# The second output-weight tile of a gated MLP, split in two and laid at other byte offsets

## The chip, the cores and the metric

The kernel runs on one core of a Trainium2 chip, in float32. The time is that of one execution on the device, in microseconds. The profile is one further execution, recorded by the hardware profiler; its span runs from the first to the last instruction that it shows. The engines are named as in the profile: PE multiplies matrices, PEld is its loading of weights (the operand that stays in the array, 128 columns at a time, while the other one streams past), DVE and ACT work on vectors, POOL and SP here mostly issue DMA transfers.

## What is computed

A linear attention feeds a gated MLP. Shapes: q, k, v are 8 x 8 x 576 x 64; the MLP has 4608 tokens, width 512, hidden width 1536. The weights arrive as 64-bit floats and are narrowed on the chip.

```python
def _attn_ref(q, k, v):
    q_s = np.exp(q - np.max(q, axis=-1, keepdims=True))
    q_s = q_s / (np.sum(q_s, axis=-1, keepdims=True) + 1e-09)
    k_s = np.exp(k - np.max(k, axis=2, keepdims=True))
    k_s = k_s / (np.sum(k_s, axis=2, keepdims=True) + 1e-09)
    kv = np.einsum('bhsd,bhse->bhde', k_s, v)
    return np.einsum('bhsd,bhde->bhse', q_s, kv)

def _moe_ref(x, w_gate, w_val, w_out):          # x: attention, as 4608 x 512
    gate = 1.0 / (1.0 + np.exp(-(x @ w_gate)))
    return (gate * (x @ w_val)) @ w_out
```

## The kernel before

The tokens go in nine windows of 512 (T). Window 0 multiplies in plain float32 while the weights are read and prepared (g1_0 at L672, g2_0 at L699). Windows 1 to 8 multiply in float32r, a form in which a matmul streams its 512 columns faster; to keep the precision each operand is held as a high part and a low part, and a product is three matmuls: high by high, and high by low both ways.

Each of these windows has six steps, one for each pair of hidden blocks of 128 columns (NS = 6, step, at, p). A step has these parts, in program order:

- g1 (L717): the first layer for this pair, 84 matmuls of 256 columns in seven products (a Strassen scheme, prod). Its weights are a_w, which stays in SBUF, and s_sb, sums of weights that POOL loads again for the next step as each product is done (s_load, L301). What streams is c_hl, the window's attention output.
- On ACT and DVE: sigmoid, gate times value, and h_split (L767, L768), which makes the high and the low part of the pair's hidden values, h.
- side_a and side_b: attention work for the next window, some of it on PE (k_mm at L424 between g1 and g2 in one step of a window, x_mm at L587 behind g2 in the last).
- g2 (L785) of the step before: the second layer, 24 matmuls of 512 columns. For both blocks of the pair (i), for each of four token blocks (m), three matmuls. The operand that is loaded as weights is a 128-column slice of h; what streams is the output weights of that block, wo_hl for the first block and wo_t for the second.
- wo_load (L248), on POOL's queue: the output weights for the next step. Two tiles of 512 KB, each [128, 2, 512]: high part, then low part. The first comes from whpool (named wo_hl in the profile), the second from wtpool (wo_t). Each pool has two buffers, so a step is loaded while another is in use. The first step of window 1 takes both of its tiles from whpool, straight from where they were made (wo_out).

PE takes its matmuls in program order; the schedule is written by hand (manual_schedule). In window 0, wtpool also holds the narrowed output weights in float32 (wo_top, wo_join, two blocks to a tile), from which wo_hi and wo_lo make the high and the low part and wo_store sends them to DRAM (wo_dram).

What matters for the change is where in SBUF a tile begins. The pools lie one behind another in the order in which they are opened. The tiles of all pools around the change are multiples of 512 bytes per partition, and three pads stand between them: pad_w (128 bytes) in wpad, pad_h (128) in hpad, pad_f (64) in fpad. So, modulo 512, wo_t begins 128 bytes behind h, wo_hl 256 behind h, and the ring of attention tiles 320. h, a_w, s_sb and kv_sb, which are loaded as weights, all begin at the same place modulo 512; c_hl begins 448 bytes behind it. The slices that a matmul loads or streams start at multiples of 512 within their tiles, so each has its tile's offset.

Of the kernel before, what the change touches and what calls it, by code (L numbers as in the profile page):

```python
# [8 lines left out]
F32 = mybir.dt.float32  # L9
F32R = mybir.dt.float32r  # L10
# [4 lines left out]
ALU = mybir.AluOpType  # L15
AX = mybir.AxisListType

P = 128
B, H, S, D = 8, 8, 576, 64
DM, DF = 512, 1536  # L20
# [6 lines left out]
NJ = DF // P  # L27
NK = DM // P
NS = NJ // 2
# [22 lines left out]
def attn_moe(ctx: ExitStack, tc: tile.TileContext, qf, qn, qT, k, kT, v, wg, wv, wo, out):  # L52
    nc = tc.nc
# [8 lines left out]
    apool = ctx.enter_context(tc.tile_pool(name="apool", bufs=1))  # L62
    two = ctx.enter_context(tc.tile_pool(name="two", bufs=2))
    wpad = ctx.enter_context(tc.tile_pool(name="wpad", bufs=1))
    wtpool = ctx.enter_context(tc.tile_pool(name="wtpool", bufs=2))
    hpad = ctx.enter_context(tc.tile_pool(name="hpad", bufs=1))
    whpool = ctx.enter_context(tc.tile_pool(name="whpool", bufs=2))
    fpad = ctx.enter_context(tc.tile_pool(name="fpad", bufs=1))
    four = ctx.enter_context(tc.tile_pool(name="four", bufs=4))
# [19 lines left out]
    wo_dram = [spool.tile([P, 2 * DM], F32, name=f"wo_{j}") for j in range(NJ)]  # L89
# [3 lines left out]
        out=kv_sb.rearrange("p b i h e -> p (b i) (h e)"),  # L93
        in_=kv_0.rearrange("p h e -> p (h e)").unsqueeze(1).broadcast_to([P, 4, DM]),
# [19 lines left out]
    wo_raw = {}  # L114
    f_w = {}
    a_w = {}
    wo_t = {}
# [22 lines left out]
    def words(raw):  # L140
        return raw.rearrange("p (e two) -> p e two", two=2)
# [8 lines left out]
    def narrow_sign(raw):  # L150

        half = raw.bitcast(F16).rearrange("p (e f) -> p e f", f=4)
        nc.scalar.activation(
            half[:, :, 1], words(raw)[:, :, 1].bitcast(F32), AF.Copy, scale=2.0 ** -100
        )
# [8 lines left out]
    def narrow_abs(raw, w):  # L164
        src = words(raw)[:, :, 1].bitcast(F32)
        if len(w.shape) == 3:
            src = src.rearrange("p (a b) -> p a b", a=w.shape[1])
        nc.scalar.activation(w, src, AF.Abs, scale=2.0 ** -112)

    def narrow_join(raw, w):  # L170
        bits = w.bitcast(I32)
        low = words(raw)[:, :, 0]
        if len(w.shape) == 3:
            low = low.rearrange("p (a b) -> p a b", a=w.shape[1])
        nc.vector.scalar_tensor_tensor(
            out=bits, in0=bits, scalar=3, in1=low,
            op0=ALU.logical_shift_left, op1=ALU.bitwise_or,
        )
# [23 lines left out]
    def wo_on_vector(j):  # L202
        return j % 2
# [4 lines left out]
            narrow_sign_bits(wo_raw[j])  # L208

    def wo_top(j):  # L210
        if j % 2 == 0:
            wo_t[j // 2] = wtpool.tile([P, 2, DM], F32, name="wo_t")
        if not wo_on_vector(j):
            narrow_sign(wo_raw[j])
        narrow_abs(wo_raw[j], wo_t[j // 2][:, j % 2])

    def wo_join(j):
        narrow_join(wo_raw.pop(j), wo_t[j // 2][:, j % 2])

    wo_out = {}  # L220

    def wo_hi(j):
        wo_out[j] = t = whpool.tile([P, 2, DM], F32R, name="wo_hl")
        nc.scalar.copy(out=t[:, 0], in_=wo_t[j // 2][:, j % 2])

    def wo_lo(j):
        t = wo_out[j]
        nc.vector.tensor_tensor(
            out=t[:, 1], in0=wo_t[j // 2][:, j % 2], in1=t[:, 0].bitcast(F32), op=ALU.subtract
        )  # L230

    def wo_store(j):
        t = wo_out[j]
        nc.gpsimd.dma_start(out=wo_dram[j], in_=t.rearrange("p h e -> p (h e)").bitcast(F32))
# [5 lines left out]
    wo_hl = {}  # L240

    def wo_load(w, p):
        wo_hl[w, p] = [
            pool.tile([P, 2, DM], F32R, name=tag)
            for pool, tag in ((whpool, "wo_hl"), (wtpool, "wo_t"))
        ]
        for i, t in enumerate(wo_hl[w, p]):
            nc.gpsimd.dma_start(  # L248
                out=t.rearrange("p h e -> p (h e)"), in_=wo_dram[2 * p + i].bitcast(F32R)
            )  # L250

    s_32 = {}

# [401 lines left out]
    def c_split(i):  # L655
        c_split_hi(i)
        c_split_lo(i)


    acc = {}  # L660


    h_0 = {}
# [22 lines left out]
    def acc_new(w):  # L686
        acc[w] = [ps_acc.tile([P, DM], F32, name="acc") for _ in range(NT)]

    def acc_out(w):
        for m in range(NT):  # L690
            nc.scalar.copy(out=x_32[:, m], in_=acc[w][m])  # L691
            nc.sync.dma_start(out=out[w * T + m * P:w * T + (m + 1) * P], in_=x_32[:, m])
        del acc[w]

    def g2_0(j):
        if j == 0:
            acc_new(0)
        for m in range(NT):
            nc.tensor.matmul(  # L699
                acc[0][m], lhsT=h_0[j][:, m * P:(m + 1) * P], rhs=wo_t[j // 2][:, j % 2],  # L700
                start=(j == 0), stop=(j == NJ - 1),
            )
        if j == NJ - 1:
            acc_out(0)
# [57 lines left out]
    def h_split(w, p):  # L762
        h_hl[w, p] = hi, lo = [
            two.tile([P, 2, T], F32R, name="h", tag=f"h_{x}") for x in ("hi", "lo")
        ]
        hi, lo = (t.rearrange("p i (q t) -> p (i q) t", q=2) for t in (hi, lo))
        nc.vector.tensor_copy(out=hi, in_=sg[:, :, 0])  # L767
        nc.vector.tensor_tensor(  # L768
            out=lo, in0=sg[:, :, 0], in1=hi.bitcast(F32), op=ALU.subtract
        )  # L770


    def step(w, i):
        return (i - 1) % NS if w == 1 else i

    def g2(w, at):
        p = step(w, at)
        if at == 0:
            acc_new(w)
        h, o = h_hl.pop((w, p)), wo_hl.pop((w, p))  # L780
        for i in range(2):
            for m in range(NT):
                sl = slice(m * P, (m + 1) * P)
                for lh, rh in ((0, 0), (0, 1), (1, 0)):
                    nc.tensor.matmul(  # L785
                        acc[w][m], lhsT=h[lh][:, i, sl], rhs=o[i][:, rh],
                        start=(at == 0 and i == 0 and lh == 0 and rh == 0),
                        stop=(at == NS - 1 and i == 1 and lh == 1),
                    )
        if at == NS - 1:  # L790
            acc_out(w)
# [3 lines left out]
    def side_a(n, p):  # L795

        b = n if n < B else None
        if p == 0:
            for c in range(NC):
                qn_max(n, c)  # L800
            qn_send(n, "m")
            for c in range(NC):
                qn_sub(n, c)
            if b is not None:
                k_sub(b, 0); k_sub(b, 1)
                k_sum(b, 2); k_sum(b, 3)
        if p == 1:
            if b is not None:
                for t in range(2, 5):
                    k_sub(b, t)  # L810
            for c in range(NC):
                qn_exp(n, c)
            if b is not None:
                for t in range(5):
                    k_exp(b, t)
            for c in range(NC):
                qn_sum(n, c)
        if p == 2:
            if b is not None:
                for t in range(5):  # L820
                    k_mm(b, t)
                k_done(b)
            for hp in range(NP):
                qT_sub(n, hp)
        if p == 3:
            for hp in range(NP):
                qT_exp(n, hp)
        if p == 4:
            for hp in range(NP):
                qT_split(n, hp)  # L830
# [193 lines left out]
    for j in range(NJ - 2):  # L1024
# [31 lines left out]
        if j > 0:  # L1056
            g2_0(j - 1)
# [4 lines left out]
    j = NJ - 2  # L1062
# [15 lines left out]
    g_mul_0(j)  # L1078
    wo_join(j + 1)
    g2_0(j - 1)  # L1080

    g1_0(j + 1)
# [22 lines left out]
    wo_hi(j + 1)  # L1105
    wo_lo(j + 1)
    g2_0(j)
    for t in range(2, 5):
        v_load(2, t)

    def wo_next(w, at):
        wo_load(w, step(w, at))

    prev = None
    for w in range(1, NW):
        last = w == NW - 1
        for at in range(NS):
            p = step(w, at)
            end = last and at == NS - 1
            g1(w, p, None if end else step(w + (at + 1) // NS, (at + 1) % NS))  # L1120
            if prev is None:
                wo_store(NJ - 1)
            ahead = 3 if at == NS - 1 and not last else 0
            for i in range(ahead):
                c_split(i)
            h_split(w, p)
            if ahead:
                for i in range(ahead, 7):
                    c_split(i)
            if not last:  # L1130
                side_a(w + 1, at)
            if prev is None:
                g2_0(NJ - 1)
                wo_hl[1, NS - 1] = [wo_out[j] for j in (NJ - 2, NJ - 1)]
            else:
                g2(*prev)
                if prev == (1, 0):
                    wo_next(1, 1)
                if not end:
                    wo_next(w + (at + 1) // NS, (at + 1) % NS)  # L1140
            prev = (w, at)
            if not last:
                side_b(w + 1, at)
    g2(*prev)


# [36 lines left out]
```

## Time and profile before

| | |
|---|---|
| time, median of 3 runs | 928.67 us (928.15 to 929.54) |
| the profiled execution's own time | 928.82 us |
| its span | 927.1 us |
| instructions | 16312 |
| PE busy with L785, wo_hl (588 matmuls) and wo_t (564) | 142.6 and 138.9 us |
| PE busy with L717, s_sb (2304) and a_w (1728) | 277.5 and 220.9 us |
| DMA | 256.77 MB, mean 277 GB/s |

A row of the timeline gives the start of a group in us from the span's start, the time from its first start to its last end, the engine, the line, the operation, the tiles that it writes and reads, the shapes and the count. Matmuls overlap: each one's recorded duration is longer than its distance to the next, so a pace is read from starts. A row of the chain of waits gives start, duration and what ran. In a grouped row, busy time and the mean duration of one (in ns) stand behind the first bar, the engine's idle time ahead of it behind the second. A row of waits names who waited, for whom, the sum in us, how often, and the longest.

### The profile page before, as it was taken

Reading aid. Unit: us, or ns where it says so; the run is one execution under the profiler, and the core shown is the slowest. Engines: PE = TensorE matmul, PEld = TensorE weight load, DVE = VectorE, ACT = ScalarE, POOL = GpSimd, SP = SyncE. Lnnn points to the kernel's source line nnn. Section 1 sums busy time; section 2 is a strip of 40 time slices with the busy share of each in tenths; the row PEclk is TensorE's granted clock in tenths of the full one; section 3 lists DMA queues with packets and bytes.
Section 4 is the critical chain, followed back from the end, with each engine's and each line's share of the span. In section 5 each row is a group of like instructions: output and inputs, shape, how many; then the busy total and the mean of one; then the engine's idle time right before and its main releaser. Section 6 shows DMA issues by size and latency. Waiting matters only on the chain.

```text
span 927.1 us, 16312 instructions
## 1 busy us (share of the span) xinstructions
PE 919.4 (99%) x6366; PEld 793.9 (86%) x6366; DVE 619.1 (67%) x1005; ACT 488.7 (53%) x830; POOL 177.2 (19%) x329
## 2 busy tenths in 40 slices
PE   8999999999999999999999999999999999999998
PEld 7445445899999999999999999999999999899997
DVE  7899889865768476757775677656855574654232
ACT  5999885735454544644564456444634443543222
POOL 0011113222121212121221222112211222122220
PEclk9999999999999999999999999999999999999999
DMA  9996676999799969996999699969997799768661
GB/s 331 380 376 255 238 269 238 360 340 283 205 373 323 273 192 372 334 281 183 360 342 282 200 333 333 300 203 310 334 298 219 222 260 317 227 190 257 209 206 68
DMA packets 92507, 256.77 MB, mean 277 GB/s; under 512 B 13648, under 2 KB 13648, under 8 KB 92432
## 3 DMA queue, kind: packets, MB, share of 16 engines
q0 software_dynamic: 46016, 167.27, 57.8%
q1 hardware_dynamic: 46416, 88.48, 31.5%
q8 instruction: 50, 0.82, 0.4%
q14 instruction: 25, 0.20, 0.1%
HBM read 227.15 MB, written 28.56 MB: 276 GB/s over the span
## 4 chain that ended last, share of the span: by engine, by line
PE 98%; DMA 1%; SPq 0%; ACT 0%; issue 0%
PE gv L717 49%; PE acc L785 29%; PE gv L672 9%; PE acc L699 4%; PE at L424 2%; PE gv L587 2%; PE at L587 1%; DMA lent<-v_in 1%; DMA lent<-qf_in 1%; PE gv L549 0%; PE acc L611 0%; PE acc L410 0%; PE at L410 0%; SPq L948 0%; SPq L951 0%; ACT x L691 0%
## 5 line engine op out<-in xcount | busy, mean ns | idle before, releaser
L717 PE MATMUL gv<-c_hl,s_sb 128*128 128x256 f32 x2304 | 277.5, 276 | 0.0
L717 PEld LDWEIGHTS gv<-c_hl,s_sb 128*128 128x128 f32 x2304 | 269.0, 188 | 0.0
L717 PE MATMUL gv<-c_hl,a_w 128*128 128x256 f32 x1728 | 220.9, 277 | 0.0
L717 PEld LDWEIGHTS gv<-c_hl,a_w 128*128 128x128 f32 x1728 | 210.4, 188 | 4.6 <-issue 0.7
L301 POOL DMA_DIRECT2D s_sb<-s x188 | 101.7, 541 | 305.6 <-PE gv L717 297.9
L785 PE MATMUL acc<-wo_hl,h 128*128 128x512 f32 x588 | 142.6, 391 | 0.0
L743 DVE TENSOR_TENSOR sg<-gv,sg 128x512 f32<-128x512 f32 x48 | 33.2, 691 | 158.8 <-PE gv L717 158.8
L785 PE MATMUL acc<-wo_t,h 128*128 128x512 f32 x564 | 138.9, 394 | 0.0
L785 PEld LDWEIGHTS acc<-wo_t,h 128*128 128x128 f32 x564 | 105.8, 188 | 24.8
L785 PEld LDWEIGHTS acc<-wo_hl,h 128*128 128x128 f32 x588 | 106.9, 188 | 20.5
L735 ACT COPY sg<-gv 128x512 f32<-128x512 f32 x48 | 28.1, 586 | 111.0 <-PE gv L717 97.7
L745 ACT COPY sg<-gv 128x512 f32<-128x512 f32 x48 | 28.2, 588 | 102.7 <-PE gv L717 102.7
L747 DVE TENSOR_TENSOR sg<-sg 128x512 f32<-128x512 f32 x48 | 33.3, 693 | 57.3 <-ACT sg L745 57.3
L672 PE MATMUL gv<-x,f_w 128*128 128x512 f32 x160 | 70.4, 593 | 0.0
L248 POOL DMA_DIRECT2D wo_hl<-wo x47 | 27.7, 590 | 182.6 <-PE acc L785 182.6
L672 PEld LDWEIGHTS gv<-x,f_w 128*128 128x128 f32 x160 | 30.0, 190 | 36.6 <-issue 34.4
L768 DVE TENSOR_TENSOR h<-sg,h 128x1024 fp32r<-128x1024 f32 x48 | 58.9, 1226 | 1.6
L756 DVE TENSOR_TENSOR sg<-sg 128x512 f32<-128x512 f32 x48 | 33.3, 693 | 33.6 <-ACT sg L750 33.6
L750 ACT ACTIVATE sg<-sg 128x512 f32<-128x512 f32 x48 | 30.4, 633 | 46.1 <-DVE sg L749 46.1
L740 ACT COPY sg<-gv 128x512 f32<-128x512 f32 x48 | 28.2, 588 | 37.3 <-PE gv L717 37.3
L737 ACT COPY sg<-gv 128x512 f32<-128x512 f32 x48 | 28.2, 588 | 36.3 <-PE gv L717 36.3
L248 POOL DMA_DIRECT2D wo_t<-wo x47 | 25.4, 540 | 99.1 <-PE acc L785 99.0
(148 smaller groups left out, 1120.8 us busy)
## 6 DMA issues: line engine op xcount, KB each, us to landing
s_sb<-s POOLq DMA_DIRECT2D x188, 512.0 KB, 6.4
wo_hl<-wo POOLq DMA_DIRECT2D x47, 512.0 KB, 4.3
wo_t<-wo POOLq DMA_DIRECT2D x47, 512.0 KB, 6.1
s<-s_sb POOLq DMA_DIRECT2D x24, 512.0 KB, 6.9
out<-x SPq DMA_DIRECT2D x36, 256.0 KB, 6.9
ring<-k_in SPq DMA_DIRECT2D x28, 256.0 KB, 8.8
ring<-qn_in SPq DMA_DIRECT2D x28, 256.0 KB, 5.9
q_b<-q_m_row SPq DMA_DIRECT2D x56, 128.0 KB, 9.6
```

Source lines behind the costliest of these rows:

```text
L248: nc.gpsimd.dma_start(out=t.rearrange("p h e -> p (h e)"), in_=wo_dram[2 * p + i].bitcast(F32R))
L301: nc.gpsimd.dma_start(out=s_sb[:, i].rearrange("p h n e -> p (h n e)"), in_=s_dram[p][:, i * n:(i + 1) * n].bitcast(F32R),)
L672: nc.tensor.matmul(ps[n], lhsT=w[:, kt // 2, sl], rhs=x_0[:, kt], start=(kt == 0), stop=(kt == NK - 1),)
L699: nc.tensor.matmul(acc[0][m], lhsT=h_0[j][:, m * P:(m + 1) * P], rhs=wo_t[j // 2][:, j % 2], start=(j == 0), stop=(j == NJ - 1),)
L717: nc.tensor.matmul(ps[:, n], lhsT=lh(kt), rhs=c_hl[i][:, x, kt], start=(first and n == 0 and kt == 0 and lh is wh and x == 0), stop=(last ...
L737: nc.scalar.copy(out=sg[:, 2], in_=z)
L743: nc.vector.tensor_tensor(out=sg[:, 0], in0=rr, in1=sg[:, 0], op=ALU.add)
L747: nc.vector.tensor_tensor(out=sg[:, 3], in0=sg[:, 3], in1=sg[:, 2], op=ALU.add)
L750: nc.scalar.activation(sg[:, 0:2, 0], sg[:, 0:2, 0], AF.Sigmoid)
L756: tt(out=sg[:, 0:2, 0], in0=sg[:, 0:2, 0], in1=sg[:, 0:2, 1], op=ALU.mult)
L768: nc.vector.tensor_tensor(out=lo, in0=sg[:, :, 0], in1=hi.bitcast(F32), op=ALU.subtract)
L785: nc.tensor.matmul(acc[w][m], lhsT=h[lh][:, i, sl], rhs=o[i][:, rh], start=(at == 0 and i == 0 and lh == 0 and rh == 0), stop=(at == NS - ...
```

## The change

The second tile of a step's output weights becomes two tiles of [128, 512]: its high part, still from wtpool (wo_t), and its low part from a new pool, wlpool (wo_l). The pools are opened in another order: wpad, wlpool, hpad, wtpool, whpool. Modulo 512, wo_l then begins 128 bytes behind h, and wo_t and wo_hl 256. wo_load issues three transfers for a step instead of two. In g2 the order of the three matmuls changes for both blocks, so that the one with the low part of the output weights comes last, where it stood second. In window 0 the even blocks of the narrowed weights lie in wtpool, the odd ones in wlpool, instead of two to a tile.

```diff
     wpad = ctx.enter_context(tc.tile_pool(name="wpad", bufs=1))
+    wlpool = ctx.enter_context(tc.tile_pool(name="wlpool", bufs=2))
+    hpad = ctx.enter_context(tc.tile_pool(name="hpad", bufs=1))
     wtpool = ctx.enter_context(tc.tile_pool(name="wtpool", bufs=2))
-    hpad = ctx.enter_context(tc.tile_pool(name="hpad", bufs=1))
     whpool = ctx.enter_context(tc.tile_pool(name="whpool", bufs=2))
...
     def wo_top(j):
-        if j % 2 == 0:
-            wo_t[j // 2] = wtpool.tile([P, 2, DM], F32, name="wo_t")
+        pool, name = ((wtpool, "wo_t"), (wlpool, "wo_l"))[j % 2]
+        wo_t[j] = pool.tile([P, DM], F32, name=name)
         if not wo_on_vector(j):
             narrow_sign(wo_raw[j])
-        narrow_abs(wo_raw[j], wo_t[j // 2][:, j % 2])
+        narrow_abs(wo_raw[j], wo_t[j])
...
     def wo_load(w, p):
-        wo_hl[w, p] = [
-            pool.tile([P, 2, DM], F32R, name=tag)
-            for pool, tag in ((whpool, "wo_hl"), (wtpool, "wo_t"))
+        t = whpool.tile([P, 2, DM], F32R, name="wo_hl")
+        nc.gpsimd.dma_start(
+            out=t.rearrange("p h e -> p (h e)"), in_=wo_dram[2 * p].bitcast(F32R)
+        )
+        parts = [
+            pool.tile([P, DM], F32R, name=name) for pool, name in ((wtpool, "wo_t"), (wlpool, "wo_l"))
         ]
-        for i, t in enumerate(wo_hl[w, p]):
+        for h, o in enumerate(parts):
             nc.gpsimd.dma_start(
-                out=t.rearrange("p h e -> p (h e)"), in_=wo_dram[2 * p + i].bitcast(F32R)
+                out=o, in_=wo_dram[2 * p + 1][:, h * DM:(h + 1) * DM].bitcast(F32R)
             )
+        wo_hl[w, p] = [[t[:, h] for h in range(2)], parts]
...
-                for lh, rh in ((0, 0), (0, 1), (1, 0)):
+                for lh, rh in ((0, 0), (1, 0), (0, 1)):
                     nc.tensor.matmul(
-                        acc[w][m], lhsT=h[lh][:, i, sl], rhs=o[i][:, rh],
+                        acc[w][m], lhsT=h[lh][:, i, sl], rhs=o[i][rh],
                         start=(at == 0 and i == 0 and lh == 0 and rh == 0),
-                        stop=(at == NS - 1 and i == 1 and lh == 1),
+                        stop=(at == NS - 1 and i == 1 and rh == 1),
                     )
...
-                wo_hl[1, NS - 1] = [wo_out[j] for j in (NJ - 2, NJ - 1)]
+                wo_hl[1, NS - 1] = [
+                    [wo_out[j][:, h] for h in range(2)] for j in (NJ - 2, NJ - 1)
+                ]
```

wo_join, wo_hi, wo_lo and g2_0 read wo_t[j] in place of wo_t[j // 2][:, j % 2].

More of the change, by code (lines that the diff above doesn't have):

```diff
@@ L210, in wo_top @@
     def wo_top(j):
-        if j % 2 == 0:
-            wo_t[j // 2] = wtpool.tile([P, 2, DM], F32, name="wo_t")
+        pool, name = ((wtpool, "wo_t"), (wlpool, "wo_l"))[j % 2]
+        wo_t[j] = pool.tile([P, DM], F32, name=name)
         if not wo_on_vector(j):
             narrow_sign(wo_raw[j])
-        narrow_abs(wo_raw[j], wo_t[j // 2][:, j % 2])
+        narrow_abs(wo_raw[j], wo_t[j])
     def wo_join(j):
-        narrow_join(wo_raw.pop(j), wo_t[j // 2][:, j % 2])
+        narrow_join(wo_raw.pop(j), wo_t[j])
     wo_out = {}
@@ L223, in wo_hi @@
         wo_out[j] = t = whpool.tile([P, 2, DM], F32R, name="wo_hl")
-        nc.scalar.copy(out=t[:, 0], in_=wo_t[j // 2][:, j % 2])
+        nc.scalar.copy(out=t[:, 0], in_=wo_t[j])
     def wo_lo(j):
@@ L228, in wo_lo @@
         nc.vector.tensor_tensor(
-            out=t[:, 1], in0=wo_t[j // 2][:, j % 2], in1=t[:, 0].bitcast(F32), op=ALU.subtract
+            out=t[:, 1], in0=wo_t[j], in1=t[:, 0].bitcast(F32), op=ALU.subtract
         )
@@ L699, in g2_0 @@
             nc.tensor.matmul(
-                acc[0][m], lhsT=h_0[j][:, m * P:(m + 1) * P], rhs=wo_t[j // 2][:, j % 2],
+                acc[0][m], lhsT=h_0[j][:, m * P:(m + 1) * P], rhs=wo_t[j],
                 start=(j == 0), stop=(j == NJ - 1),
```

## The prediction

> **What bounds the kernel now.** I read the page first: share of each engine, granted clock, chain.
>
> ```profile
> span 927.1 us, 16312 instructions
> PE 919.4 (99%) x6366; PEld 793.9 (86%) x6366; DVE 619.1 (67%) x1005; ACT 488.7 (53%) x830; POOL 177.2 (19%) x329
> PEclk9999999999999999999999999999999999999999
> PE 98%; DMA 1%; SPq 0%; ACT 0%; issue 0%
> ```
>
> The matrix engine works from end to end at its full granted clock, and the chain that ended last is PE for 98%. Then the waits of PE, all of them:
>
> ```profile
> PE acc L394 <- ACT lent L337: 2.2, 2, 1.9
> PE gv L975 <- POOL lent L943: 1.1, 1, 1.1
> PE at L410 <- DMA lent<-v_in: 0.3, 1, 0.3
> ```
>
> 3.6 us in total, all in the prologue. So no load, no VectorE step and no buffer holds PE up in the 48 steps; what is left to win or lose is the pace at which matmuls follow each other. A busy PE hides that, so I read starts in the timeline. One step of the middle (start, duration, count; durations overlap, so the start of the next row is what counts):
>
> ```profile
> 405.41 2.90 PE L785 MATMUL acc<-wo_hl,h 128*128 128x512 f32 x12
> 408.15 2.95 PE L785 MATMUL acc<-wo_t,h 128*128 128x512 f32 x12
> 410.94 1.52 PE L717 MATMUL gv<-c_hl,a_w 128*128 128x256 f32 x12
> 412.30 2.88 PE L717 MATMUL gv<-c_hl,s_sb 128*128 128x256 f32 x24
> ...
> 420.46 2.90 PE L785 MATMUL acc<-wo_hl,h 128*128 128x512 f32 x12
> ```
>
> The twelve matmuls of the first tile (wo_hl, 256 bytes behind the weights modulo 512) take 408.15 - 405.41 = 2.74 us, the twelve of the second (wo_t, 128 behind) 410.94 - 408.15 = 2.79 us: 228.3 against 232.5 ns each, for the same work and the same shapes. The first step of the window loop has both of its tiles in wo_hl:
>
> ```profile
> 178.96 5.62 PE L785 MATMUL acc<-wo_hl,h 128*128 128x512 f32 x24
> 184.42 1.58 PE L717 MATMUL gv<-c_hl,a_w 128*128 128x256 f32 x12
> ```
>
> 5.46 us for 24, 227.5 each, against 5.53 in the step above. The offset is thus worth up to 0.07 us a step, and 47 steps have it: 3.3 us is all that the second tile can lose. But the chain of waits shows what follows that step (start, duration, what):
>
> ```profile
> 179.13 5.46 PE acc L785 x24
> 184.58 9.89 PE gv L717 x84
> 197.10 5.78 PE acc L785 x24
> 202.88 9.52 PE gv L717 x84
> 212.40 5.53 PE acc L785 x24
> 217.93 9.52 PE gv L717 x84
> ...
> 902.47 9.52 PE gv L717 x84
> ```
>
> The next product of the first layer (L717, 84 matmuls, the same in every step) takes 9.89 us behind the step that ended at 256 and 9.52 behind steps that ended at 128, with no wait in either. In the timeline its first twelve take 185.83 - 184.42 = 1.41 us against 412.30 - 410.94 = 1.36. So the pace has a memory: a run of matmuls settles into a rhythm that the end of the run before chose, and keeps it.
>
> **How the pace goes, matmul by matmul.** The rows above merge twelve starts. Read singly in the trace, they repeat to the nanosecond. In wo_hl behind L717 they lie 231, 233, 231 and then nine times 226.7 ns apart (2.735 us, the 2.74 of the row). In wo_t they lie 234 and 224, and then alternate 237.5 and 229 (2.79 us). The tail shows that going back from 128 to 256 costs what coming from L717 costs:
>
> ```profile
> 914.56 2.96 PE L785 MATMUL acc<-wo_t,h 128*128 128x512 f32 x12
> 917.35 2.90 PE L785 MATMUL acc<-wo_hl,h 128*128 128x512 f32 x12
> 920.09 2.96 PE L785 MATMUL acc<-wo_t,h 128*128 128x512 f32 x12
> ```
>
> 920.09 - 917.35 is 2.74 again, 0.015 us over twelve steady ones, all in the first three. The starts also show what state is carried: each falls on one of a few places in a beat of 6.67 ns (226.7 is 34 beats, 237.5 + 229 is 70), and the place and the offset decide the next distance.
>
> **The change, part by part.**
>
> *Offsets.* Of the 12 second-tile matmuls of a step, 8 move to 256 and 4 stay at 128, in the order 256, 256, 128, four times. The first tile only changes the order of its products; both h tiles are at one offset, so its pace stays. Priced by each matmul's own offset: 8 x 226.7 + 4 x 232.5 = 2.744 us for 2.79, 0.046 us a step. But a change of offset has a price too, and there are seven instead of one. A pair at 256 that comes from 128 is the first two of the tail's entry, 231 + 233 = 464 instead of 453; a 128 behind it takes 229 from the place where that entry stands after two. That round (231.7, 232.5, 229.2) closes on itself, at 104 beats: 693 ns for three, where wo_t now takes 3 x 233.3 = 700. The first three start from the steady 256: 226.7 x 2 + 234 = 687. Sum: 13 ns for the first and 6.7 for each of the other three, 0.033 us, or 0.026 if the second three must first find the round. I take 0.026, since the trace has no 256 right behind a single 128: 47 x 0.026 = 1.2 us less. Bounds: 47 x 0.07 = 3.3 us less if 128 costs nothing among 256s, a little more if its 224 comes back (four times 224 for 226.7, another 0.5 us); and if every second-tile matmul goes at the worst of its pairs, (238 + 234 + 233)/3 = 235 for 232.5, 47 x 12 x 2.5 ns = 1.4 us more.
>
> *What runs behind.* L717 now starts behind a 128 in steady alternation; of the 39 products that follow an L785 directly, 38 take the 9.52 pace (the first of them at 202.88, the last at 902.47; 184.58 is the other). In the round above the last 128 ends on the same place of the beat as now, so I leave L717 at 9.52. Seven times a run, attention products (L587) stand between:
>
> ```profile
> 236.41 9.89 PE gv L717 x84
> 332.98 9.55 PE gv L717 x84
> 811.83 9.89 PE gv L717 x84
> ```
>
> Two of the seven leave L717 slow today, and a new start may flip any: from 2 x 0.37 = 0.7 us less to 5 x 0.35 = 1.8 more. Taken as nothing.
>
> *The third transfer.* Each load of a step becomes three issues on POOL instead of two, 47 x 0.54 us, behind the end of L785:
>
> ```profile
> 411.40 0.54 POOL L248 DMA_DIRECT2D wo_t<-wo  x1 [2.24 <-PE acc L785]
> 414.12 0.54 POOL L301 DMA_DIRECT2D s_sb<-s  x1 [2.18 <-PE gv L717]
> s_sb<-s POOLq DMA_DIRECT2D x188, 512.0 KB, 6.4
> wo_t<-wo POOLq DMA_DIRECT2D x47, 512.0 KB, 6.1
> ```
>
> The low tile's issue waits, like the high tile's, for the last matmuls of the group; queued behind it is the load of the sums. POOL idles 2.18 us before that, so 0.54 fits. The tile is read two steps of 15.05 us (405.41 to 420.46) behind 408.15, 26.8 us after the issue, and lands in 6.1: nothing. Without that cover the load of the sums would come 0.54 us later in each step. 47 x 0.52 of the software queue's 167 MB now come in rows of 2 KB instead of 4; the two queues show what that costs:
>
> ```profile
> q0 software_dynamic: 46016, 167.27, 57.8%
> q1 hardware_dynamic: 46416, 88.48, 31.5%
> ```
>
> 57.8% of 16 x 927.1 us over 46016 packets is 186 ns for one of 3.6 KB; likewise 101 ns for one of 1.9 KB. Two cost about as much as one: nothing.
>
> *Order.* h's low part is wanted at the second matmul, 0.23 us earlier. Only the last step is near: its subtraction starts at 914.18 and the group at 917.35.
>
> ```profile
> 914.18 1.23 DVE L768 TENSOR_TENSOR h<-sg,h 128x1024 fp32r<-128x1024 f32 x1
> ```
>
> Done at 915.41, 1.9 us ahead: nothing.
>
> *Window 0.* Its L699 reads the even tiles at 256 instead of 128.
>
> ```profile
> L672 PE MATMUL gv<-x,f_w 128*128 128x512 f32 x160 | 70.4, 593 | 0.0
> L699 PE MATMUL acc<-wo_t,h 128*128 128x512 f32 x96 | 43.1, 592 | 0.0
> ```
>
> L672 has another offset (448) and the same 592 to 593 ns: plain float32 shows no offset. Nothing.
>
> Sum: 928.82 us, the profiled execution's own time (its span and 1.7 us around it), less 1.2 is 927.6; that execution stands 0.15 over the median 928.67, so 927.5.
>
> **A rule that speaks against it.** The Trainium skill, "TensorE: Matmul & The Clock Gate", Part 2, step 1, says that PE has two independent read ports, so that loading the next weights takes nothing from the running matmul. By that rule no offset could matter and the sum would be nothing, 928.7. The trace disagrees: 2.74 against 2.79 us for equal work.
>
> **The rivals.**
>
> *Low parts ride free* (0.23). If two matmuls at 256 bring the rhythm back each time, the second tile costs its own offsets or less: 2.1 to 3.9 us less, 926.6 to 924.8. For it: steady places are sticky. Against: in the rows above three matmuls are needed, not two.
>
> *Switches eat the gain* (0.11). Each triple keeps 700 ns or more, up to the 1.4 us above and a flip or two behind L587: 928.5 to 930.4. For it: 234 is the dearest distance but one, and every round would have it.
>
> *Offsets do nothing* (0.03). The 0.05 us between the tiles then belongs to being second in the group: 928.7. Against it: the step with 24 from wo_hl, whose second twelve are as quick as its first. (This is what the Trainium skill's rule on the two read ports comes to.)
>
> *L717 falls into the slow pace* (0.20, the other side). If the last 128 ends on another place than now, each following product takes 9.89: 38 x 0.37 = 14 us more, less 0.6 saved at the entries into wo_hl and the 1.2 of the tile: 941. It decides in one place, the end of each step, and there as good as always or never, since steps repeat. For it: the step that ended at 256, and a single 128 leaves two 256s little time to be forgotten. Against: the last matmul is a 128, and 38 of 38 ends at 128 were fast. A few steps only (0.03): 930.5 to 934.
>
> **How the numbers follow.** Forecast 0.40 at 927.5, with its own range 926.4 to 928.5, rivals as above. The range 924.8 to 930.6 leaves out the slow pace. A measurement of this kernel can tell about 0.2% from no change, 1.9 us: below 926.8 lie the free ride and an edge of the forecast, 0.27; above 930.5 the slow pace, whole or in part, 0.23; within, 0.50.
>
> **What would show it.** In the chain, L785 x24 at 5.50 instead of 5.53 (5.46 for the free ride), and L717 x84 at 9.52; 9.89 behind most steps is the slow pace. In the timeline the second tile's starts should span 2.765 us. A PE wait on wo_t or its low-part tile would break the third-transfer step. I am wrong outright if the place where a matmul starts depends on more than place and offset.

## The result and the profile after

The changed kernel takes 940.7 us (median of 4 runs, 940.0 to 941.0) where the kernel before takes 929.1 (928.2 to 932.3, the three runs of the table above and a fourth): a ratio of 1.0129 over the fast runs, with a 95% interval of 1.0113 to 1.0146. The forecast was 927.5, with a range of 924.8 to 930.6. The rival that ends on the other side, L717 in its slow pace, had 941.

First the page of the changed kernel. Line numbers have moved by five: the first layer (L717) is now L722, the second (L785) L790, the attention product (L587) L592.

```profile
span 938.7 us, 16449 instructions
PE 930.4 (99%) x6366; PEld 806.2 (86%) x6366; DVE 618.5 (66%) x1005; ACT 488.0 (52%) x830; POOL 201.5 (21%) x376
PEclk9999999999999999999999999999999999999999
L722 PE MATMUL gv<-c_hl,s_sb 128*128 128x256 f32 x2304 | 285.8, 280 | 0.0
L722 PE MATMUL gv<-c_hl,a_w 128*128 128x256 f32 x1728 | 227.1, 281 | 0.0
L790 PE MATMUL acc<-wo_hl,h 128*128 128x512 f32 x588 | 142.2, 391 | 0.0
```

PE is busy for 930.4 us with the same 6366 matmuls and the same granted clock. The growth stands in the two rows of L722, whose operands keep their offsets: 285.8 and 227.1 us where L717 had 277.5 and 220.9, 14.5 us more. wo_hl has the 142 us that it had. The waits of PE have not grown to match:

```profile
PE acc L399 <- ACT lent L342: 2.1, 2, 1.5
PE gv L980 <- POOL lent L948: 1.1, 1, 1.1
PE at L415 <- DMA lent<-v_in: 0.9, 3, 0.4
```

4.1 us in all, again in the prologue. So nothing waits for the third transfer. The chain of waits (start, duration, what) shows where the time is:

```profile
184.15 9.89 PE gv L722 x84
194.05 2.63 PE at L429 x80
196.67 5.73 PE acc L790 x24
202.41 9.89 PE gv L722 x84
212.30 5.47 PE acc L790 x24
217.77 9.89 PE gv L722 x84
227.66 5.47 PE acc L790 x24
233.13 2.58 PE gv L592 x18
235.70 0.86 PE at L592 x6
236.57 9.53 PE gv L722 x84
...
898.46 9.89 PE gv L722 x84
908.35 5.47 PE acc L790 x24
913.82 9.89 PE gv L722 x84
923.71 10.95 PE acc L790 x48
```

Each product behind a second layer takes 9.89 us, from the first to the last; the second layer itself takes 5.47 instead of 5.53. The sum: 38 products that went from 9.52 to 9.89 are 14.1 us, 47 second layers at 0.06 less are 2.8 back, and behind L592 three products of the seven are slow instead of two, 0.4. That is about 11.7, and the span grew by 938.7 - 927.1 = 11.6.

The timeline of one step shows the second tile:

```profile
408.46 2.88 PE L790 MATMUL acc<-wo_hl,h 128*128 128x512 f32 x12
411.18 0.62 PE L790 MATMUL acc<-wo_t,h 128*128 128x512 f32 x2
411.63 0.40 PE L790 MATMUL acc<-wo_l,h 128*128 128x512 f32 x1
411.87 0.61 PE L790 MATMUL acc<-wo_t,h 128*128 128x512 f32 x2
...
413.69 0.40 PE L790 MATMUL acc<-wo_l,h 128*128 128x512 f32 x1
413.93 1.57 PE L722 MATMUL gv<-c_hl,a_w 128*128 128x256 f32 x12
415.34 2.99 PE L722 MATMUL gv<-c_hl,s_sb 128*128 128x256 f32 x24
```

Two matmuls at 256 take 411.63 - 411.18 = 0.45 us, the one at 128 behind them 0.24, and the twelve 413.93 - 411.18 = 2.75. Read singly, the starts lie 227, 226 and 234 ns apart, four times over: 687 ns a round, 103 beats of 6.67. wo_hl, 411.18 - 408.46 = 2.72, starts straight in its steady pace. Then twelve matmuls of L722 take 1.41 us, the slow pace, against 1.36 before.

Last, POOL, at the end of the same step:

```profile
414.15 0.54 POOL L252 DMA_DIRECT2D wo_t<-wo  x1 [1.98 <-PE acc L790]
414.68 0.54 POOL L252 DMA_DIRECT2D wo_l<-wo  x1
417.21 0.54 POOL L306 DMA_DIRECT2D s_sb<-s  x1 [1.99 <-PE gv L722]
```

The third issue ends at 415.22, and POOL idles 1.99 us before the load of the sums, which waits for PE and not for it.

### The profile page after: what moved, and what is told of

It reads as the page before. It is cut to its first block, busy times and chain, and to the rows that moved or that the text cites. A ratio compares the mean times of both kernels' runs of the same rounds, so it can differ in the third digit from the quotient of the medians.

```text
span 938.7 us, 16449 instructions
## 1 busy us (share of the span) xinstructions
PE 930.4 (99%) x6366; PEld 806.2 (86%) x6366; DVE 618.5 (66%) x1005; ACT 488.0 (52%) x830; POOL 201.5 (21%) x376
## 4 chain that ended last, share of the span: by engine, by line
PE 92%; DMA 4%; DVE 3%; issue 0%; ACT 0%; SPq 0%; DVEq 0%
PE gv L722 50%; PE acc L790 28%; PE gv L677 5%; PE acc L704 3%; PE at L429 2%; PE gv L592 2%; DMA sg<-wg_in 1%; PE at L592 1%; DMA wo_raw<-wo_in 1%; DMA ring<-qf_in 1%; DMA lent<-v_in 1%; DMA lent<-qf_in 0%; DVE ring L380 0%; DVE ring L507 0%; DVE f_w L176 0%
## 5 line engine op out<-in xcount | busy, mean ns | idle before, releaser
L722 PE MATMUL gv<-c_hl,s_sb 128*128 128x256 f32 x2304 | 285.8, 280 | 0.0
L722 PEld LDWEIGHTS gv<-c_hl,s_sb 128*128 128x128 f32 x2304 | 277.2, 189 | 0.0
L722 PE MATMUL gv<-c_hl,a_w 128*128 128x256 f32 x1728 | 227.1, 281 | 0.0
L722 PEld LDWEIGHTS gv<-c_hl,a_w 128*128 128x128 f32 x1728 | 216.3, 189 | 4.4 <-issue 0.7
L790 PE MATMUL acc<-wo_hl,h 128*128 128x512 f32 x588 | 142.2, 391 | 0.0
L790 PEld LDWEIGHTS acc<-wo_hl,h 128*128 128x128 f32 x588 | 107.0, 188 | 20.2
L790 PE MATMUL acc<-wo_t,h 128*128 128x512 f32 x376 | 115.6, 389 | 0.0
L790 PEld LDWEIGHTS acc<-wo_t,h 128*128 128x128 f32 x376 | 70.5, 187 | 15.6
L790 PE MATMUL acc<-wo_l,h 128*128 128x512 f32 x188 | 74.3, 395 | 0.0
```

The costliest lines, as they stand in the source:

```text
L722: nc.tensor.matmul(ps[:, n], lhsT=lh(kt), rhs=c_hl[i][:, x, kt], start=(first and n == 0 and kt == 0 and lh is wh and x == 0), stop=(last ...
L790: nc.tensor.matmul(acc[w][m], lhsT=h[lh][:, i, sl], rhs=o[i][rh], start=(at == 0 and i == 0 and lh == 0 and rh == 0), stop=(at == NS - 1 a ...
```

## The experiments

What was to be settled: why L722 is slow. The beat theory says that L722 settles into one of two rhythms, and that the place in the beat at which the last second-layer matmul ends picks it. Its rivals: the third transfer or its short rows (transfer theory), the new order of the products (order theory), or the number of matmuls at 128 in a row at the end (last-run theory).

**The order alone, and the offsets with the old order.** The first kernel is the changed one with the three products as they were:

```diff
-                for lh, rh in ((0, 0), (1, 0), (0, 1)):
+                for lh, rh in ((0, 0), (0, 1), (1, 0)):
...
-                        stop=(at == NS - 1 and i == 1 and rh == 1),
+                        stop=(at == NS - 1 and i == 1 and lh == 1),
```

> The changed kernel with the old order of the three products (the low-part product second, a high-part product at offset 256 last). Beat theory (what the next L717 does is chosen by the place of the beat at which the last second-layer matmul ends, and both orders end at a place that is not that of the long alternation at 128): second tile 2.73 to 2.74 us, L717 x84 at 9.89 behind most steps, 940 us. Order theory (the new order itself, low part last, disturbs L717): back to 9.52 and 927 to 929 us. Transfer theory (the third POOL transfer or its 2 KB rows slow L717): 9.89, 941 us.

The second is the kernel before with the opposite edit.

> The kernel before with only the new order of the three products; its second tile stays one tile at 128. Beat theory: every address sequence is as before, so 2.79 us for the second tile, 9.52 for L717 x84, the time of before within 0.1%. Order theory: 9.89 and some 941 us. Transfer theory: as before.

Measured: 939.7 us, 1.0122 of before (1.0105 to 1.0139), for the first; 927.8, 0.9993 (0.9981 to 1.0005), for the second. Their chains, first the changed kernel with the old order, then the kernel before with the new one:

```profile
211.34 5.47 PE acc L790 x24
216.80 9.89 PE gv L722 x84
```

```profile
212.83 5.53 PE acc L785 x24
218.36 9.52 PE gv L717 x84
```

The order does nothing by itself, and bringing the old one back cures nothing: the order theory is out.

**The split without the offsets.** Pools in other orders put both new tiles at 128, or both at 256. Both at 128:

```diff
     wlpool = ctx.enter_context(tc.tile_pool(name="wlpool", bufs=2))
-    hpad = ctx.enter_context(tc.tile_pool(name="hpad", bufs=1))
     wtpool = ctx.enter_context(tc.tile_pool(name="wtpool", bufs=2))
+    hpad = ctx.enter_context(tc.tile_pool(name="hpad", bufs=1))
```

> The changed kernel, three transfers and new order, but with both new tiles 128 bytes behind the weights modulo 512 (the second pad behind them). Beat theory: 2.79 us for the second tile, 9.52 for L717 x84, the time of before within 0.1%: the split and the third transfer cost nothing. Transfer theory: 9.89 and 941 us.

Both at 256 has hpad ahead of wlpool:

```diff
+    hpad = ctx.enter_context(tc.tile_pool(name="hpad", bufs=1))
     wlpool = ctx.enter_context(tc.tile_pool(name="wlpool", bufs=2))
-    hpad = ctx.enter_context(tc.tile_pool(name="hpad", bufs=1))
     wtpool = ctx.enter_context(tc.tile_pool(name="wtpool", bufs=2))
```

> The changed kernel with both new tiles at 256 (both pads ahead of them). Beat theory: as in the step of before that had 24 matmuls at 256, second tile 2.72 us, L717 x84 at 9.89, 940 us, some 0.6 us less than the changed kernel. Transfer and order theories: 9.89 as well; this run tells whether the single matmuls at 128 had any part in the slow pace.

Measured: 928.0 us, 1.0002 (0.9992 to 1.0011), at 128; 940.3, 1.0134 (1.0111 to 1.0158), at 256. The chain of the one at 128, then of the one at 256:

```profile
211.34 5.53 PE acc L790 x24
216.87 9.52 PE gv L722 x84
```

```profile
213.60 5.44 PE acc L790 x24
219.04 9.89 PE gv L722 x84
```

With the split, the third transfer and the new order, but the whole second tile at 128, the time of before is back: the transfers cost nothing that can be measured. With all of it at 256 the second layer is quickest, 5.44, and L722 is slow, without any 128 in the step. The whole loss is in the offsets; it is not the mixing of two of them.

**How many at 128 come last.** The three products of each token block are kept, but in the last n token blocks of the second tile the low-part products wait until all the high-part ones are done, so that a step ends with n matmuls at 128:

```diff
-        for i in range(2):
-            for m in range(NT):
...
-                for lh, rh in ((0, 0), (1, 0), (0, 1)):
+        todo = [(0, m, *x) for m in range(NT) for x in ((0, 0), (1, 0), (0, 1))]
+        todo += [
+            (1, m, *x) for m in range(NT) for x in ((0, 0), (1, 0), (0, 1))[:2 if m >= NT - LAST else 3]
+        ]
+        todo += [(1, m, 0, 1) for m in range(NT - LAST, NT)]
+        for i, m, lh, rh in todo:
```

LAST is 2, 4 and 3.

> The changed kernel with the second tile's products in another order: two groups of three as they were, then the four high-part products of the last two token blocks, then their two low-part products, so that each step ends with two matmuls at 128. Beat theory: by the distances read in before (the first matmul at 128 behind a settled 256 takes 234 ns and ends off the place, the second takes 224 and ends on the place from which L717 goes fast), second tile 2.74 us, L717 x84 at 9.52 behind it, 926 us, 0.9973 of before. Last-run theory (L717 goes fast only behind a long run at 128, as the twelve of before): 9.89, 940 us.

> All eight high-part products of the second tile first, then the four low-part ones. Beat theory: 234, 224, 237.5, 229 and the place of before: second tile 2.74 us, 9.52 for L717 x84, 926 us, 0.9973 of before, the same as with two last. Last-run theory: between, faster than with two last if four are enough.

> One group of three as it was, six high-part products, then three low-part ones. Beat theory: 234, 224, 237.5 end on the other place of the alternation; near that place L717 went slow where it came behind L587 in before (at 236.41 and 811.83), so 9.89 behind most steps and 940 us, slow between two fast neighbours (two and four last). Last-run theory: between two and four last, no slower than with two last.

| matmuls at 128 in a row at the end | product behind it, us | time, us | of before |
|---|---|---|---|
| 1 (the changed kernel) | 9.89 | 940.7 | 1.0129 (1.0113 to 1.0146) |
| 2 | 9.52 | 926.3 | 0.9989 (0.9977 to 1.0001) |
| 3 | 9.90 | 942.3 | 1.0152 (1.0138 to 1.0166) |
| 4 | 9.52 | 927.5 | 0.9992 (0.9983 to 1.0001) |
| 12 (the kernel before) | 9.52 | 928.2 | 1 |

The chain with two last, then with three last:

```profile
211.18 5.47 PE acc L794 x24
216.65 9.52 PE gv L722 x84
226.17 5.47 PE acc L794 x24
```

```profile
211.77 5.50 PE acc L794 x24
217.27 9.90 PE gv L722 x84
227.17 5.50 PE acc L794 x24
```

Slow, fast, slow, fast: more matmuls at 128 don't help as such; of the numbers tried, the even ones are fast. The last-run theory can't give that; the alternation does, since from the second on every second matmul at 128 ends on the same place. The order of the token blocks changed in these three as well, but three last, slow between two and four, speaks against that as the cause. The timeline with two last shows the pair:

```profile
407.66 1.07 PE L794 MATMUL acc<-wo_t,h 128*128 128x512 f32 x4
408.56 0.62 PE L794 MATMUL acc<-wo_l,h 128*128 128x512 f32 x2
409.02 1.52 PE L722 MATMUL gv<-c_hl,a_w 128*128 128x256 f32 x12
410.38 2.88 PE L722 MATMUL gv<-c_hl,s_sb 128*128 128x256 f32 x24
```

409.02 - 408.56 = 0.46 us for the two (234 and 224 ns singly), against 0.45 for two at 256, and then twelve of L722 in 1.36. This version has the quick tile and the fast product. It beats the changed kernel by 1.5%; against the kernel before, its interval just holds 1, as that of four last does, so a gain is not shown. The 0.9973 expected of both lies below both intervals.

**One at 256 behind twelve at 128.** The kernel before, with the last product of the first tile moved to the end:

```diff
+        todo = [(i, m, *x) for i in range(2) for m in range(NT) for x in ((0, 0), (0, 1), (1, 0))]
+        todo.append(todo.pop(11))
+        for k, (i, m, lh, rh) in enumerate(todo):
```

> The kernel before, second tile wholly at 128, but the last product of the first tile (at 256) is moved to the end of the group, so that each step ends with one matmul at 256 behind twelve at 128. Beat theory: that matmul takes 232 ns and ends four places further, where L717 came from behind L587 at 718.68 in before and found its fast pace after some five matmuls: L717 x84 at 9.53 to 9.56, 929 to 930 us. Last-offset theory (what ends at 256 is slow): 9.89 behind each step, 942 us.

Measured: 943.5 us, 1.0165 (1.0151 to 1.0179). The timeline:

```profile
411.62 2.95 PE L785 MATMUL acc<-wo_t,h 128*128 128x512 f32 x12
414.42 0.39 PE L785 MATMUL acc<-wo_hl,h 128*128 128x512 f32 x1
414.65 1.57 PE L717 MATMUL gv<-c_hl,a_w 128*128 128x256 f32 x12
416.06 2.99 PE L717 MATMUL gv<-c_hl,s_sb 128*128 128x256 f32 x24
```

The moved matmul takes the 0.23 us expected of it (414.65 - 414.42), and L717 then goes slow, 1.41 us for twelve. Here the forecast from the beat theory missed, and "what ends at 256 is slow" had 942; but that rule says nothing for the changed kernel and the one with three last, which end at 128 and are slow. The forecast leaned on a product of the kernel before that came behind L587 and was fast after five matmuls:

```profile
718.68 9.63 PE gv L717 x84
```

By its starts that product did not come from the same place. Count places in eighths of the beat, from the place that the settled matmuls at 256 keep all through a run; single starts, in whole ns, tell a place to about 0.6 of an eighth. In the kernel before, L717 at 718.68 has its first start on 6.6; here L717 starts on 4. Behind a second layer the 38 products of each run start on one place, each within 0.6 of the number given:

| kernel | place of the first start, eighths of the beat | product, us |
|---|---|---|
| before; before with the new order; both at 128; two last; four last | 6 | 9.52 |
| one at 256 behind twelve at 128 | 4 | 9.89 |
| three last | 3 | 9.90 |
| the changed kernel | 1 | 9.89 |
| the changed kernel with the old order; both at 256 | 0 | 9.89 |

So 6 is fast, and 0, 1, 3 and 4 are slow. The two products of the kernel before that were slow behind L587 (at 236.41 and 811.83) start on 3.6 and 3.5, which fits the slow 4. Even so the place alone is not the whole state: the product at 236.57 in the changed kernel, behind L592, starts on 0 and is fast (9.53), where all 76 that start on 0 behind a second layer are slow. Something of the matmul ahead counts too; what it is was not found.

**The offset of the first layer's own operand.** Do the two rhythms of L722 belong to its own offset of 448, so that the end of the second layer only picks one of them (the theory of two sides below)? Three kernels are the changed one with the two pools that hold c_hl opened elsewhere, so that c_hl begins 256, 128 or 0 bytes behind the weights instead of 448; all other tiles keep their offsets modulo 512. For 256:

```diff
-    bpool = ctx.enter_context(tc.tile_pool(name="bpool", bufs=1))
-    cpool = ctx.enter_context(tc.tile_pool(name="cpool", bufs=1))
...
     whpool = ctx.enter_context(tc.tile_pool(name="whpool", bufs=2))
+    bpool = ctx.enter_context(tc.tile_pool(name="bpool", bufs=1))
+    cpool = ctx.enter_context(tc.tile_pool(name="cpool", bufs=1))
     fpad = ctx.enter_context(tc.tile_pool(name="fpad", bufs=1))
```

For 128 they stand ahead of hpad, for 0 ahead of the pool named two.

> The changed kernel with the streamed operand of L717 (the c_hl tiles) 256 bytes behind the weights instead of 448; the pools of c_hl are opened behind whpool, everything else keeps its offset. Theory of two sides (the two rhythms of L717 belong to its own offset of 448, the end of the second layer only picks one): L717 x84 leaves 9.89 for another length, the same behind every step: 9.4 to 9.5 and 926 us if 256 has a fast rhythm alone, 9.9 or more and 941 us or more if it has a slow one alone. One-sided theory (a step that ends off the place slows whatever comes next): 9.89 and 941 us as in the changed kernel.

> The same with c_hl 128 bytes behind the weights. Theory of two sides: its own length, not that of 448 or 256, if each offset has its own rhythms; as the second layer's twelve matmuls at 128 take longer than those at 256, slower than with 256. One-sided theory: 9.89 and 941 us.

> The same with c_hl at the weights' own offset (0). Theory of two sides: its own length again; nothing in the float32r rows of before has this offset, so faster and slower than 9.52 are both open. One-sided theory: 9.89 and 941 us.

Measured: 951.7 us (1.0256, 1.0239 to 1.0273), 946.2 (1.0201, 1.0185 to 1.0217) and 952.2 (1.0262, 1.0247 to 1.0278). Chains at 256, at 128 and at 0:

```profile
218.56 10.07 PE gv L722 x84
```

```profile
221.34 9.97 PE gv L722 x84
```

```profile
218.63 10.07 PE gv L722 x84
```

The length goes with the offset of L722's own operand; 0 and 256 give the same. Of the four offsets only 448 has shown 9.52. The theory of two sides holds, but its guess that 128 would be slower than 256, by likeness with the second layer, was wrong.

## Why the prediction was wrong

What held: nothing but the pace of the matmuls bounds the loop, 38 products stood to lose 0.37 us each, and the third transfer, the order and h's low part cost nothing. The rival of the slow pace had the mechanism and the price (941), and was given 0.20.

The step that failed is the one on what runs behind: "In the round above the last 128 ends on the same place of the beat as now, so I leave L717 at 9.52." It stood on the step before it, the choice of the round. I put together a round from distances read elsewhere (231.7, 232.5, 229.2; the pair at 256 from the tail's entry) because the trace had no 256 right behind a single 128. The runs show another: 227, 226, 234. The 256 behind a single 128 takes 226 ns and falls back on the settled place, so each last 128 is the first one out of that place: L722 starts on 1, where it goes slow, and not on 6 as L717 did. The sum of the first three, 226.7 x 2 + 234, already ended on 1 (234 is one eighth over 35 beats), and the round that was priced closes on itself only from 6, where the tail's entry begins. The 38 of 38 fast ends that were set against the rival were all ends on one place. Had I asked what each place does to L717, and not only which place my round reached, the two ends that I knew to be fast or slow (behind twelve at 128, behind 24 at 256) would have covered one place each, with every other unknown; 0.20 for them together was too little.

The term of the tile was mis-sized the other way: 0.026 us a step forecast, 0.044 measured (2.748 for 2.79), about the least that the rival of the free ride gave it. With 0.015 more saved at wo_hl's entry this is the 0.06 between 5.53 and 5.47.

"I am wrong outright if the place where a matmul starts depends on more than place and offset": the product at 236.57 of the changed kernel, fast from place 0, is a sign that for L717 it does.

The Trainium skill, "TensorE: Matmul & The Clock Gate", Part 2, step 1, has it that loading the next weights takes no read bandwidth from the running matmul, as PE reads through two ports. The prediction read this as a rule by which no offset could matter; the runs disagree with that reading: with c_hl at 448, 128 or 256 behind the weights and every other offset kept, the same 84 matmuls take 9.52 or 9.89, 9.97 and 10.07 us. Whether read bandwidth is the reason, no run here shows.

What stays open: what the beat is, why one place gives the fast rhythm and others the slow one, and what of the matmul ahead counts beside its place.

## What to carry to other kernels

Where matmuls follow each other without a gap, don't price a change of layout by the matmuls that read the moved tile: the next group may keep for its whole length a rhythm that the last few chose, and here 0.06 us won in 24 matmuls cost 0.37 in the 84 behind them. Before such a change, list how each kind of group starts behind each end that the trace holds, and count every end that it doesn't hold as open. A reorder of the last matmuls can keep the gain of an offset and the rhythm behind it, as with two last (5.47 and 9.52).

## What the runs showed of the hardware

- The distance of float32r matmuls depends on where the streamed tile begins against the weights: settled at 226.7 ns at 256, at 229 and 237.5 in turn at 128, for 512 columns (2.72 and 2.79 us for twelve); for 84 of 256 columns 10.07 us at 0 and at 256, 9.97 at 128, 9.52 or 9.89 at 448. Plain float32 showed no such thing (in window 0 of the changed kernel most starts lie 429 ns apart, with wo_t at 256 and with wo_l at 128 alike).
- At 448 there are two rhythms, 113.3 and 117.7 ns a matmul (9.52 and 9.89 over 84), and a group may keep either to its end. Behind matmuls of 512 columns the place of its first start goes with the rhythm: 6 eighths of the beat of 6.67 ns fast, 0, 1, 3 and 4 slow. So the number of matmuls at 128 behind a settled 256 decides: 1, 3 slow, 2, 4, 12 fast.
- The output weights' second tile in two transfers with 2 KB rows instead of one with 4 KB rows, 47 transfers more, left the time as it was (both at 128: 1.0002, 0.9992 to 1.0011).
